# A gated linear attention followed by a snake layer: two stages in a row, against both interleaved chunk by chunk

## The chip, the cores and the metric

The kernel runs on one core of one Trainium2 chip. The metric is the device time of one execution in microseconds (us); an execution is timed as a whole, and a profile of one execution tells what each engine did in it. The engines are TensorE (PE, with its weight loads PEld), VectorE (DVE), ScalarE (ACT), GpSimd (POOL) and SyncE (SP), which here only issues DMAs. Each engine works through its own instructions in order and waits on semaphores that others raise.

## The reference

Inputs are float32: q, k, v and f_logit of 4 batches x 8 heads x 768 positions x 48, and the weights of a layer with 384 inputs and 2048 hidden units. The output is 3072 x 384.

```python
f = 1.0 / (1.0 + np.exp(-f_logit))
for t in range(S):
    state = f[:, :, t, :, None] * state + np.einsum('bhd,bhe->bhde', k[:, :, t], v[:, :, t])
    y[:, :, t] = np.einsum('bhd,bhde->bhe', q[:, :, t], state)
x = np.ascontiguousarray(attn_out.transpose(0, 2, 1, 3)).reshape(B * S, H * D)
h = x @ w_in
s = np.sin(alpha * h)
g = h + s * s / (alpha + 1e-09)
return (g @ w_out).astype(np.float32)
```

The recurrence is computed in chunks of 128 positions. With G the running product of f inside the chunk (exp of a running sum of logarithms), q is multiplied by G and k by 1/G; inside the chunk the result is a masked product of the two with v, and what came before enters through a 48 x 48 state per head that is carried from chunk to chunk.

## The kernel before

It runs two stages one after the other, with a DRAM scratch between them.

**Stage one, attention** (lines 80 to 160). Six chunks, each with all 32 heads (4 batches x 8) side by side. Per chunk, four loads of 768 KB bring f, v, q and k, positions on the partitions. ACT takes the sigmoid (L102) and its logarithm (L104). PE forms the running sums with a triangular mask, 512 columns at a time (L112), DVE copies them out (L113), ACT takes exp of plus and minus the sums (L116, L118), DVE multiplies q and k (L120, L122). A product with a column of ones (L127) and an exp (L128) give each head's decay over the chunk. Then a loop runs over the 32 heads: two transposes (L137, L141) that DVE copies out (L139, L143), the product of k and q (L146) that DVE masks (L148), two products that add up in one PSUM bank (L151 with v, L152 with the state), a DVE copy (L154) and a DMA of 12 KB into the scratch (L155), and the new state (L158, then DVE L159, L160). Each of these instructions serves a single head, so it uses 48 of the 128 rows or columns of the array and short rows on DVE.

**Stage two, the snake layer** (lines 162 to 196). Three DMAs bring the scratch back as x, transposed (L172). Six blocks of 512 tokens follow, each with 16 hidden blocks `fb` of 128 units: three matmuls of 512 columns make `h_ps` (L182, four PSUM buffers), ACT takes the sine with alpha as a per-partition scale (L186) and the square with 1/sqrt(alpha) as scale (L187), DVE adds h (L189), and four matmuls of 384 columns add up the four output tiles (L191). At the block's end DVE copies these out (L195) and SP stores them (L196).

The weights are loaded whole and cast to bf16 by DVE before stage one starts (L74 to L78). The order of the work on each engine is set by the framework's scheduler, from the order of the code and the buffers that are free. A pool's `bufs` is the number of buffers that a tile's name rotates through: a tile can be written only once the readers of the one that had the buffer are done.

## Time and profile before

| what | us |
|---|---|
| time, median of 2 runs (493.24 and 493.69) | 493.47 |
| span of the profiled execution, first to last instruction | 490.3 |
| PE busy in it | 389.7 |
| DVE busy | 316.4 |
| ACT busy | 207.6 |
| POOL busy | 1.1 |

The span is what the rows of a trace add up to; the execution's time has some 3 us around it. The busy times are sums over stages that differ: in the first about 24 us nothing but the weights is loaded and cast, until 332 us stage one runs, until 343 us x is read back, and the rest is stage two. An engine's busy time over the whole span therefore says little, and the stages have to be read one by one. A busy PE is one that has some matmul in flight, not one at its peak.

### The profile page before, as it was taken

The page shows a single profiled execution, that of the slowest core. Times are in us where ns is not written, and L with a number is a line of the kernel's source. Part 1 is how long each engine was busy: PE and PEld are TensorE (multiplying, and loading weights), DVE is VectorE, ACT ScalarE, POOL GpSimd, SP SyncE. Part 2 cuts the span into 40 slices and gives each one's busy share as a digit, 9 for nine tenths or more (in the row PEclk, how much of TensorE's full clock was granted, in tenths as well). Part 3 has the DMA queues.
Part 4 walks back from the last instruction along what each step waited for, and adds up shares of the span by engine and source line. Part 5 has one row for each costly group of instructions (what it writes and reads, how often), then busy time and mean ns, then how long its engine had stood idle before and what let it go on. Part 6 is the DMA issues. An engine that isn't in the chain of part 4 may idle for free.

```text
span 490.3 us, 6888 instructions
## 1 busy us (share of the span) xinstructions
PE 389.7 (79%) x2016; PEld 189.6 (39%) x2034; DVE 316.4 (65%) x1343; ACT 207.6 (42%) x429; POOL 1.1 (0%) x9
## 2 busy tenths in 40 slices
PE   0004999499949994999499959994799999999994
PEld 0002544344425442554255434541344444444441
DVE  1515888688867886788678868881346565555553
ACT  1057303621075105300500040000799999999993
POOL 0000000000000000000000000000000000000000
PEclk9999999999999999999999999999999999999998
DMA  8699558947586642500000000005001010110101
GB/s 281 233 183 187 83 87 135 132 74 127 89 143 104 98 76 51 91 11 12 4 10 10 13 4 10 12 11 197 0 0 66 1 66 0 66 44 22 49 17 65
DMA packets 119430, 35.07 MB, mean 72 GB/s; under 512 B 113504, under 2 KB 118624, under 8 KB 119008
## 3 DMA queue, kind: packets, MB, share of 16 engines
q1 hardware_dynamic: 119392, 34.63, 36.1%
q8 instruction: 16, 0.26, 0.2%
q14 instruction: 22, 0.18, 0.1%
HBM read 27.53 MB, written 7.08 MB: 71 GB/s over the span
## 4 chain that ended last, share of the span: by engine, by line
PE 58%; ACT 18%; issue 8%; DVE 7%; DMA 7%; SPq 0%; DVEq 0%; ACTq 0%
PE y_ps L151 10%; PE y_ps L152 9%; PE kT_ps L141 9%; PE at_ps L146 8%; ACT s_sb L186 7%; PE out_ps L191 7%; PE sc_ps L158 5%; PE qT_ps L137 4%; DMA wtmp_out<-in_moe_w_out_dram 4%; PE h_ps L182 3%; ACT Gl L128 3%; PE glps L127 3%; DVE g_bf L189 3%; ACT s_sb L187 2%; ACT Gi L116 2%
## 5 line engine op out<-in xcount | busy, mean ns | idle before, releaser
L189 DVE TENSOR_TENSOR g_bf<-h_ps,s_sb 128x512 bf16<-128x512 f32 x96 | 65.7, 691 | 73.5 <-ACT s_sb L187 70.0
L191 PE MATMUL out_ps<-w_out_bf,g_bf 128*128 128x384 bf16 x384 | 79.9, 332 | 9.2 <-DVE g_bf L189 7.7
L182 PE MATMUL h_ps<-xT_all,w_in_bf 128*128 128x512 bf16 x275 | 77.9, 391 | 7.1 <-issue 4.7
L154 DVE CAST yt<-y_ps 48x128 bf16<-48x128 f32 x192 | 54.3, 283 | 37.9 <-PE y_ps L152 37.9
L187 ACT ACTIVATE s_sb<-s_sb,alpha_rs 128x512 f32<-128x512 f32 x96 | 69.0, 722 | 3.0
L186 ACT ACTIVATE s_sb<-h_ps,alpha_sb 128x512 f32<-128x512 f32 x96 | 64.5, 674 | 9.8 <-PE h_ps L182 8.8
L137 PE MATMUL qT_ps<-ident,qh 128*48 128x128 bf16 x192 | 59.7, 311 | 1.6 <-DVE qh L120 1.4
L141 PE MATMUL kT_ps<-ident,kh 128*48 128x128 bf16 x192 | 57.9, 301 | 1.3 <-DVE kh L122 1.3
L152 PE MATMUL y_ps<-qtb,state 48*48 48x128 bf16 x192 | 57.4, 299 | 0.0
L146 PE MATMUL at_ps<-qtb,ktb 48*128 48x128 bf16 x192 | 54.9, 286 | 0.2
L151 PE MATMUL y_ps<-at,vt_bf 128*48 128x128 bf16 x192 | 50.9, 265 | 4.0 <-DVE at L148 3.3
L148 DVE TENSOR_TENSOR at<-at_ps,mask 128x128 bf16<-128x128 f32 x192 | 53.2, 277 | 1.1 <-PE at_ps L146 1.1
L191 PEld LDWEIGHTS <-g_bf 128*128 128x128 bf16 x384 | 30.7, 98 | 59.0 <-DVE g_bf L189 45.3
L127 PE MATMUL glps<-ones_c,ft_bf 128*48 128x1 bf16 x192 | 23.3, 168 | 30.8 <-ACT Gl L128 29.9
L128 ACT ACTIVATE Gl<-glps 48x1 f32<-48x1 f32 x192 | 22.5, 158 | 55.9 <-DVE state L160 39.4
L139 DVE COPY qtb<-qT_ps 48x128 bf16<-48x128 bf16 x192 | 39.8, 207 | 8.5 <-PE glps L127 5.6
L152 PEld LDWEIGHTS <-state 48*48 48x48 bf16 x192 | 21.5, 112 | 56.1 <-issue 55.7
L160 DVE TENSOR_SCALAR state<-state,Gl 48x48 bf16<-48x48 bf16 x192 | 42.4, 221 | 0.1
L128 ACT ACT_TABLE_LOAD x6 | 7.7, 1283 | 80.9 <-DVE state L160 80.8
L182 PEld LDWEIGHTS <-w_in_bf 128*128 128x128 bf16 x288 | 28.8, 100 | 33.7 <-issue 10.8
L143 DVE COPY ktb<-kT_ps 48x128 bf16<-48x128 bf16 x192 | 40.3, 210 | 0.7 <-PE kT_ps L141 0.4
L112 PE MATMUL gps<-ft_bf,mask 128*128 128x512 bf16 x13 | 7.5, 593 | 40.6 <-ACT ft_bf L104 35.8
(36 smaller groups left out, 326.5 us busy)
## 6 DMA issues: line engine op xcount, KB each, us to landing
ft<-in_f_logit_dram SPq DMA_DIRECT2D x6, 768.0 KB, 6.2
vt<-in_v_dram SPq DMA_DIRECT2D x6, 768.0 KB, 6.9
qt<-in_q_dram SPq DMA_DIRECT2D x6, 768.0 KB, 6.2
kt<-in_k_dram SPq DMA_DIRECT2D x6, 768.0 KB, 5.8
out_dram<-o_sb SPq DMA_DIRECT2D x24, 192.0 KB, 1.9
wtmp_in<-in_moe_w_in_dram SPq DMA_DIRECT2D x1, 3072.0 KB, 11.0
wtmp_out<-in_moe_w_out_dram SPq DMA_DIRECT2D x1, 3072.0 KB, 18.1
hgrn_x_scratch<-yt SPq DMA_DIRECT2D x192, 12.0 KB, 1.4
```

Source lines behind the costliest of these rows:

```text
L137: nc.tensor.transpose(qT_ps[:D, :], qh[:, bh, :], ident)
L141: nc.tensor.transpose(kT_ps[:D, :], kh[:, bh, :], ident)
L146: nc.tensor.matmul(at_ps[:, :C], ktb, qtb, start=True, stop=True)
L148: nc.vector.tensor_mul(at, at_ps[:, :C], mask)
L151: nc.tensor.matmul(y_ps[:D, :C], vtb, at, start=True, stop=False)
L152: nc.tensor.matmul(y_ps[:D, :C], stt, qtb, start=False, stop=True)
L154: nc.vector.tensor_copy(yt, y_ps[:D, :C])
L182: nc.tensor.matmul(h_ps, w_in_bf[:, kb, fb * P:(fb + 1) * P], xT_all[:, kb, tb * TBLK:(tb + 1) * TBLK], start=(kb == 0), stop=(kb == KB - 1))
L186: nc.scalar.activation(out=s_sb, in_=h_ps, func=Act.Sin, scale=a_sc)
L187: nc.scalar.activation(out=s_sb, in_=s_sb, func=Act.Square, scale=ai_sc)
L189: nc.vector.tensor_add(g_bf, h_ps, s_sb)
L191: nc.tensor.matmul(out_ps4[i], g_bf[:, i * P:(i + 1) * P], wout_tile, start=(fb == 0), stop=(fb == FB - 1))
```

## The change

The two stages become one loop over the six chunks. A chunk now has 128 positions of each of the 4 batches, which are 512 tokens, the size of a block of the layer.

- **Loads** are per unit of two batches (16 heads, 384 KB each of f, k, q, v), two units to a chunk, four buffers for each.
- **`pre(u)`** prepares a unit: ACT takes exp(-f) and the logarithm of one plus it (`L112`, `L113` of the changed kernel), PE sums it for eight heads at a time and puts the four per-pair decay columns beside it in the same bank (L118, L120), ACT takes both exponentials out of that bank (L124, L126), and POOL multiplies q and k and casts v (L128, L130, L114).
- **`attend(c, b)`** does the eight heads of one batch: heads stand in pairs, each padded from 48 to 64 columns, so eight transposes fill one PSUM bank and DVE empties it with one copy (L154); the masked products take two banks and two DVE instructions (L164), y one bank and two (L181, L182), the four pairs' states one (L195). The old state enters its update through a product with the identity (L187). Heads 6 and 7 of y go to a side tile `y3`, which six small DMAs put into x (L202). x stays in SBUF; the scratch is gone.
- **`mlp(c, between)`** is the layer on chunk c. Alpha is multiplied into w_in by DVE (L240) and its reciprocal into w_out by POOL (L244), so the sine and the square need no scale. Odd `fb` are squared by POOL (L265), even ones by ACT (L267). `h` has two PSUM buffers where it had four; the four output tiles are made two at a time in two banks, the second half from the 16 kept `g` tiles. The four `attend` of chunk c+1 are written between its blocks.
- After `mlp(c)` follow the two `pre` of chunk c+2. ACT keeps the order of the code (`manual_schedule`), the other engines are ordered by the scheduler. A table set with both exp and ln is loaded at the start.

```diff
-    x_scratch = nc.dram_tensor("hgrn2_x_scratch", (H, D, B, S), BF16, kind="Internal").ap()
...
-            nc.scalar.activation(out=ft, in_=ft, func=Act.Sigmoid)
-            nc.scalar.activation(out=ft_bf, in_=ft, func=Act.Ln)
...
-                h_ps = psm.tile([P, TBLK], F32, tag="hps", bufs=4)
-                nc.scalar.activation(out=s_sb, in_=h_ps, func=Act.Sin, scale=a_sc)
-                nc.scalar.activation(out=s_sb, in_=s_sb, func=Act.Square, scale=ai_sc)
...
+    ps_o = pool("ps_o", 1, space=bass.MemoryType.PSUM)
+    ps_h = pool("ps_h", 2, space=bass.MemoryType.PSUM)
+    ps_a = pool("ps_a", 4, space=bass.MemoryType.PSUM)
+    ctx.enter_context(tc.manual_schedule(engines={mybir.EngineType.Activation}))
+    nc.scalar.preload_act_table_set("natural_log_exp_and_others")
...
+    def pre(u):
+        nc.scalar.activation(out=ft, in_=ft, func=Act.Exp, scale=-1.0)
+        nc.scalar.activation(out=lf[:, :, :D], in_=ft, func=Act.Ln, bias=1.0)
+        nc.gpsimd.tensor_copy(vb[:, :, :D], vt)
+        for i in range(2):
+            nc.tensor.matmul(cs[:, :H * D], mask, lf[:, i * H:(i + 1) * H, :D], start=True, stop=True)
+            for p in range(HP):
+                nc.tensor.matmul(cs[:, H * D + p:H * D + p + 1],
...
+            nc.scalar.activation(out=G, in_=cs[:, :H * D + HP], func=Act.Exp, scale=-1.0)
+            nc.scalar.activation(out=Gi, in_=cs[:, :H * D], func=Act.Exp)
+            nc.gpsimd.tensor_mul(qh[:, hs, :D], qt[:, hs, :],
...
+            nc.gpsimd.tensor_mul(kh[:, hs, :D], kt[:, hs, :],
...
+    def attend(c, b):
+        for j, src in enumerate((kh, qh)):
+            for p in range(HP):
+                nc.tensor.transpose(tp[:, j * HP + p, :],
...
+        nc.vector.tensor_copy(tr, tp)
+        for p in range(HP):
+            for r in range(2):
+                rs = slice(r * E, (r + 1) * E)
+                nc.tensor.matmul(a_ps[r][:, p, :], tr[rs, p, :], tr[rs, HP + p, :], start=True, stop=True)
+        for r in range(2):
+            nc.vector.tensor_mul(a, a_ps[r], mask4)
...
+                    nc.tensor.matmul(y[rs, p, :], st_old[rs, p, :], tr[rs, HP + p, :],
...
+                nc.tensor.matmul(y[rs, p, :], vb[:, i * H + 2 * p + r, :], at[r][:, p, :],
...
+        nc.vector.tensor_copy(xT[:, :, ts], y[:, :KB, :])
+        nc.vector.tensor_copy(y3[:, ts], y[:, KB, :])
+                nc.tensor.matmul(kv, ident, st_old, start=True, stop=False, skip_group_check=True)
...
+                    nc.tensor.matmul(kv[rs, p, :], kh[:, hh, :], vb[:, hh, :],
...
+        if b == B - 1:
+            for r in range(2):
+                for j in range(KB):
+                    nc.sync.dma_start(out=xT[r * E + D:(r + 1) * E, j, :],
...
+        pre(0)
+        pre(1)
+        attend(0, 0)
+        attend(0, 1)
+        for g4 in range(4):
+            for j in range(KB):
+                nc.vector.tensor_mul(w_in_bf[:, j, cs_], wi[:, j, cs_], al_bc[:, cs_])
+        attend(0, 2)
+        attend(0, 3)
+        for fb in range(FB):
+            nc.gpsimd.tensor_scalar(w_out_bf[:, fb, :], wo[:, fb, :], al_r[:, fb:fb + 1], 1.0,
...
+        pre(2)
+        pre(3)
...
+        def first(fb):
+            h = ps_h.tile([P, TOK], F32, tag="h", name=f"h_{c}_{fb}")
+            for kb in range(KB):
+                nc.tensor.matmul(h, w_in_bf[:, kb, fb * P:(fb + 1) * P], xT[:, kb, :],
+                                 start=(kb == 0), stop=(kb == KB - 1))
+            nc.scalar.activation(out=s, in_=h, func=Act.Sin)
+            if fb % 2:
+                nc.gpsimd.tensor_mul(s2, s, s)
+            else:
+                nc.scalar.activation(out=s2, in_=s, func=Act.Square)
+            nc.vector.tensor_add(g, h, s2)
...
+        for fb in range(FB):
+            first(fb)
+            if fb >= 3:
+                second(os, 0, fb - 3)
+            if fb in (9, 14):
+                between.pop(0)()
...
+        for fb in range(FB):
+            second(os, 1, fb)
+            if fb in (2, 8):
+                between.pop(0)()
+        store(os, 1)
...
+        mlp(c, between)
+        if c + 2 < NCH:
+            pre(2 * c + 4)
+            pre(2 * c + 5)
```

The order of the instructions shows the change best at two places. The first is ACT. Before, it passes from the last chunk's attention into the layer once, with one table load ahead of the first sine (`Gl` is a head's decay, `s_sb` the sine and then its square):

```order
L116 ACTIVATE Gi<-glog 128x1536
L128 ACTIVATE Gl<-glps 48x1 x2
L118 ACTIVATE glog<-glog 128x1536
L128 ACTIVATE Gl<-glps 48x1 x20
L186 ACT_TABLE_LOAD
L186 ACTIVATE s_sb<-h_ps,alpha_sb 128x512 x2
L187 ACTIVATE s_sb<-s_sb,alpha_rs 128x512 x2
```

Now it passes between them at every chunk. Here ACT goes from the last sine of the second chunk through the first unit's `pre` into that of the next (`s_15` is the last sine, `f` a unit's gate, `lf` its logarithm, `cs` the sums):

```order
L262 ACTIVATE s_15_1366<-h_15_1362 128x512
L112 ACT_TABLE_LOAD
L112 ACTIVATE f_1056<-f_1056 128x768
L113 ACT_TABLE_LOAD
L113 ACTIVATE lf_92<-f_1056 128x16x48
L124 ACT_TABLE_LOAD
L124 ACTIVATE G_0_1553<-cs_0_1547 128x388
L126 ACTIVATE Gi_0_1555<-cs_0_1547 128x384
L124 ACTIVATE G_1_1565<-cs_1_1559 128x388
L126 ACTIVATE Gi_1_1567<-cs_1_1559 128x384
L112 ACTIVATE f_1064<-f_1064 128x768
L113 ACT_TABLE_LOAD
```

Three table loads stand in the first unit of the pair and two in the second, and one ahead of the next sine: six at each passage, and 26 in the program, where there were 20 (the set loaded at the start serves the first four units alone).

The second place is DVE, in the loop over heads. Before, six short instructions serve one head, in the order of the next rows, which repeats for each of the 192 head chunks:

```order
L154 CAST yt<-y_ps 48x128
L159 TENSOR_TENSOR state_109<-state_109,sc_ps 48x48
L148 TENSOR_TENSOR at<-at_ps,mask 128x128
L160 TENSOR_SCALAR state_109<-state_109,Gl 48x48
L143 COPY ktb<-kT_ps 48x128
L139 COPY qtb<-qT_ps 48x128
```

Now six longer ones serve eight heads, and the layer's additions (`g_0` to `g_4` here) stand among them. This is the start of the third chunk's layer, with `attend` of the fourth chunk's batches 0 and 1:

```order
L154 COPY tr_0_1741<-tp_0_1732 128x1024
L164 TENSOR_TENSOR at_0_0_1753<-aps_0_0_1743,mask_82 128x512
L164 TENSOR_TENSOR at_0_1_1755<-aps_0_1_1744,mask_82 128x512
L195 TENSOR_TENSOR st_0_1786<-kv_0_1776,G_0_1553 128x256
L154 COPY tr_1_1857<-tp_1_1848 128x1024
L269 TENSOR_TENSOR g_0_1624<-h_0_1616,s_2_0_1622 128x512
L269 TENSOR_TENSOR g_1_1634<-h_1_1626,s_2_1_1632 128x512
L181 CAST xT_1730<-y_0_1757 128x3x128
L182 CAST y_3_1731<-y_0_1757 128x128
L164 TENSOR_TENSOR at_1_0_1869<-aps_1_0_1859,mask_82 128x512
L269 TENSOR_TENSOR g_2_1644<-h_2_1636,s_2_2_1642 128x512
```

The additions of the first two blocks of the layer moved behind the whole of batch 0 and the transposes of batch 1, and the later ones alternate with the attention's instructions. On PE the same holds: at this passage it has the 32 matmuls of the second output half, the sums of the first unit, `h` of blocks 0 and 1, the sums of the second unit, then all of batch 0 and the first half of batch 1, and only then `h` of block 2.

More of the change, by code (lines that the diff above doesn't have):

```diff
@@ L49 @@
     ff = f_logit.rearrange("b h s d -> (b h) s d")
[L51 to L56 removed]
+    pool = lambda name, bufs, **kw: ctx.enter_context(tc.tile_pool(name=name, bufs=bufs, **kw))
+    consts = pool("consts", 1)
+    ld = pool("ld", 4)
```

277 lines of the change are left out of this document (151 added, 126 removed).

## The prediction

> **What bounds the kernel now.** I read the page first: the busy slices and the chain that ended last; then the busy times by stage; then the timeline inside each stage.
>
> ```profile
> span 490.3 us, 6888 instructions
> ...
> PE   0004999499949994999499959994799999999994
> ...
> DVE  1515888688867886788678868881346565555553
> ACT  1057303621075105300500040000799999999993
> ...
> PE 58%; ACT 18%; issue 8%; DVE 7%; DMA 7%; SPq 0%; DVEq 0%; ACTq 0%
> ```
>
> ```profile
> 0.00:30.10 30.10, 0.00 (x0) 0.10 (x1) 8.05 (x35) 1.50 (x2) 1.13 (x9) 1.00 0.83 242
> ...
> 131.00:332.00 201.00, 172.06 (x921) 88.16 (x923) 156.39 (x811) 41.87 (x148) 0.00 (x0) 1.00 0.25 40
> 332.00:343.00 11.00, 4.41 (x11) 1.49 (x12) 0.62 (x3) 0.00 (x0) 0.00 (x0) 1.00 0.63 218
> ...
> 352.00:490.00 138.00, 125.69 (x631) 55.53 (x641) 74.51 (x116) 120.00 (x183) 0.00 (x0) 0.99 0.10 35
> ```
>
> (Columns: stretch, then PE, PEld, DVE, ACT, POOL busy, clock, DMA share, GB/s.) Some 300 of the 490 us are attention, where ACT is busy a fifth of the time; 11 us are the way through DRAM; 147 us are the layer, bound by ACT at 120 of 138 us. POOL does nothing. In the attention stage PE and DVE hand one head to each other in a beat of 1.18 us (L141 to L141):
>
> ```profile
> 100.08 0.30 PE L141 MATMUL kT_ps<-ident,kh 128*48 128x128 bf16 x1
> 100.17 0.31 PE L137 MATMUL qT_ps<-ident,qh 128*48 128x128 bf16 x1
> ...
> 100.62 0.27 PE L151 MATMUL y_ps<-at,vt_bf 128*48 128x128 bf16 x1
> ...
> 100.81 0.30 PE L152 MATMUL y_ps<-qtb,state 48*48 48x128 bf16 x1
> ...
> 101.26 0.30 PE L141 MATMUL kT_ps<-ident,kh 128*48 128x128 bf16 x1
> ```
>
> 192 heads at 1.18 us are 227 us; the rest of the 300 is the preparation of six chunks. Two small matmuls start 0.09 us apart (the transposes) to 0.19 (L151, L152): the bounds for one in the new kernel.
>
> **Prices.**
>
> ```profile
> L187 ACT ACTIVATE s_sb<-s_sb,alpha_rs 128x512 f32<-128x512 f32 x96 | 69.0, 722 | 3.0
> L189 DVE TENSOR_TENSOR g_bf<-h_ps,s_sb 128x512 bf16<-128x512 f32 x96 | 65.7, 691 | 73.5 <-ACT s_sb L187 70.0 <-PE out_ps L191 3.5
> L186 ACT ACTIVATE s_sb<-h_ps,alpha_sb 128x512 f32<-128x512 f32 x96 | 64.5, 674 | 9.8 <-PE h_ps L182 8.8 <-PE out_ps L191 0.9
> L195 DVE COPY o_sb<-out_ps 128x384 f32<-128x384 f32 x24 | 12.2, 551 | 3.8 <-PE out_ps L191 2.6 <-DMA out_dram<-o_sb 1.2
> L113 DVE COPY glog<-gps 128x512 f32<-128x512 f32 x18 | 11.9, 684 | 1.7 <-PE gps L112 1.4
> L122 DVE TENSOR_TENSOR kh<-kt,Gi 128x1536 bf16<-128x1536 f32 x6 | 10.5, 1756 | 13.5 <-ACT Gi L116 13.5
> L116 ACT ACTIVATE Gi<-glog 128x1536 f32<-128x1536 f32 x6 | 8.8, 1471 | 0.0
> L59 POOL TENSOR_SCALAR_AFFINE_SELECT ident<-ident 128x128 bf16<-128x128 bf16 x1 | 0.3, 293 | 0.0
> L182 PE MATMUL h_ps<-xT_all,w_in_bf 128*128 128x512 bf16 x275 | 77.9, 391 | 7.1 <-issue 4.7
> L112 PE MATMUL gps<-ft_bf,mask 128*128 128x512 bf16 x13 | 7.5, 593 | 40.6 <-ACT ft_bf L104 35.8 <-DVE yt L154 3.8 <-DVE glog L113 0.7
> ```
>
> ACT: 128x512 costs 0.67 to 0.72 with a scale per partition, 128x1536 without one 1.47. Between them lie 0.85 for 768 columns, 0.55 for 384, and 0.65 for the sine without its scale. DVE out of PSUM: 384 columns 0.55 and 512 columns 0.68 give 1.04 ns a column and 0.15 besides, so 1.22 for the 1024-column copy, 0.69 for a mask, 0.42 for a state, 0.55 and 0.29 for y. POOL has no two-input row. From below, DVE's rate (1.756 us for 1536) gives 0.59 for 512 columns; from above, twice the affine select's rate for two inputs, 2.3. The nearest row is the affine select itself, on the same engine: 2.3 ns a column, hence 1.17 for a square and 0.88 for 384 columns, which I take.
>
> ```profile
> 346.99 2.74 PE L191 MATMUL out_ps<-w_out_bf,g_bf 128*128 128x384 bf16 x8 [2.74 <-DVE g_bf L189]
> ...
> 353.16 0.82 PE L191 MATMUL out_ps<-w_out_bf,g_bf 128*128 128x384 bf16 x4
> ...
> 357.34 0.81 PE L182 MATMUL h_ps<-xT_all,w_in_bf 128*128 128x512 bf16 x3
> ```
>
> Four output matmuls in 0.82 with the last one's 0.33 are 0.165 each; three `h` matmuls take PE 0.65 and are there after 0.81. A small matmul I take at 0.10, nearer the transposes, since most now stand in rows of eight alike.
>
> ```profile
> 31.44 1.48 ACT L102 ACTIVATE ft<-ft 128x1536 f32<-128x1536 f32 x1
> 32.94 1.28 ACT L104 ACT_TABLE_LOAD   x1
> 34.23 1.48 ACT L104 ACTIVATE ft_bf<-ft 128x1536 bf16<-128x1536 f32 x1
> ```
>
> A table load costs 1.28 and fits between its neighbours with 0.02 us to spare. The Trainium skill ("ScalarE: Activation LUTs", What ACT_TABLE_LOAD costs) adds a drain of about 1.38 us to each switch; the rows here have no room for one. By the page the 24 loads of the four passages below would add 33 us to the sum.
>
> **The change, part by part.**
>
> *Start.* DMA rates:
>
> ```profile
> 3.00:12.00 9.00, 0.00 (x0) 0.00 (x0) 0.25 (x1) 0.21 (x1) 0.00 (x0) 1.00 1.01 371
> ...
> 40.00:50.00 10.00, 5.04 (x37) 3.06 (x36) 5.55 (x14) 8.19 (x27) 0.00 (x0) 1.00 1.45 186
> ```
>
> Weights move at 371 GB/s, the gates (runs of 192 bytes) at 186. The first layer block waits, in PE's order, for the sums of unit 3, whose gate is queued behind three units (1.57 MB, 8.4 us each), the spread alpha (1 MB, 2.8, and 1 for the narrow copy), w_in and w_out (3.1 MB, 8.5 each): 2 + 25.2 + 3.8 + 17 + 2.1 = 50 us. Exp, log and sums: 52.6. Then batch 0 and most of batch 1 of the second chunk stand ahead of `h_0` (8.1 us as below, and 1.5 of state work): 62.2. Until block 2 another batch's transposes, copy, products and state follow (6.8), and `h_2`: its sine starts at 70. The first chunk's attention, the twelve w_in products on DVE and the sixteen w_out products on POOL lie under the DMAs; if they outlasted them, the cost would be their excess.
>
> *The layer loop, blocks 2 to 15.* With two `h` buffers, block n+2 may start only when block n's addition is done. For an odd block that is h 0.81 + sine 0.65 + POOL 1.17 + addition 0.69 and three or four handovers of 0.05: 3.5 us for two blocks, where ACT's own work is 2.0, and the even chain 3.0. The batches written between put into PE some 105 small matmuls (1.6 us a pair beside 2.0 of its own) and into DVE up to 1.22 at a time ahead of an addition: followed by hand, the first pairs take 3.9 and the rest 3.5. I take 3.9, since DVE's and PE's queues are in order and each delay is handed on; 6.5 pairs and a last sine are 26 us. Before, 16 blocks took 22.9 (output copy to output copy), 2.9 a pair: the layer alone gets slower, and pays for the attention that it covers.
>
> ```profile
> 393.05 1.01 DVE o_sb L195 x2
> ...
> 415.96 1.01 DVE o_sb L195 x2
> ```
>
> *The passage between chunks*, from the end of the last sine (0): POOL squares (1.2), DVE adds (1.95), PE ends the first half, DVE copies it out of the two banks that the second half needs (3.3), 32 matmuls (8.6), sums of the first unit (9.3). ACT has done three loads, exp and log by 5.5 and waits. Then 4 x 0.55 (11.5), exp (12.3), load, log (14.5), load (15.8), 4 x 0.55 (18.0), load (19.3), sines of blocks 0 and 1 and a square (21.3). PE has the second sums at 15.2, then batch 0: transposes 16.2, copy 17.4, products 18.4, masks 19.8, state matmuls 19.9, transposes of batch 1 and y 21.4; DVE: state 20.2, copy 22.2; PE: products and three of the state, 23.3; `h_2`, sine at 24.1. POOL's eight products (7 us, from 9.9) end before they are needed. The x DMAs, queued on SP behind the next loads and the output stores, start at about 4 and take 1.4 as the scratch stores did; they end under the 32 matmuls. Passage: 24 us, and with the loop 50 a round.
>
> ```profile
> hgrn_x_scratch<-yt SPq DMA_DIRECT2D x192, 12.0 KB, 1.4
> ...
> out_dram<-o_sb SPq DMA_DIRECT2D x24, 192.0 KB, 1.9
> ```
>
> *Ends.* After the fifth chunk no unit is left to prepare: its last sine to the next first one is 8.6 + 0.8 = 9.4. The sixth chunk has no batches beside it: eight pairs at 3.5, 28. Tail: first half out 1.7, 32 matmuls 5.3, two copies 1.1, store 1.9: 10.
>
> *Sum:* 70 + 4 x 50 + 26 + 9.4 + 28 + 10 = 343.4, against the span of 490.3. The median of the runs, 493.5, lies 3.2 above that span; with them the forecast is 347 us, 0.70 of the time before. The DRAM way (11 us) and the one-head beat (227) go; what is late next is the two-buffer chain and, at each passage, ACT's and PE's turns in series.
>
> **The rivals.**
>
> *B, PE becomes the bound.* At 0.2 us a small matmul (L151 to L152) a round has 184 of them, 36.8, and 20.8 of layer matmuls; with some 5 us in which PE must wait for ACT, 62. Start 72, loop of the fifth chunk 38: 72 + 248 + 38 + 10 + 28 + 10 = 406, time 409. For it: the spacing in the beat. Against it: there PE also waited for DVE.
>
> *C, the chains are shorter.* If POOL runs at DVE's rate the even chain sets 3.0 (3.4 beside batches, 22 a loop), and if pairs on different halves of the array overlap, the passage loses 2.5: 68 + 4 x 43.5 + 22 + 9 + 24 + 10 = 307, time 310. No row shows such an overlap; none excludes it.
>
> *D, the clock of PE halves: slower than before.* The eight matmuls at 346.99, after a wait, take 0.34 each against 0.165 later, though the clock column reads 1.00; L112, after a wait at each chunk, takes 593 ns where the same 512 columns take 391 in the layer. So PE runs at half speed after a pause. The passage has a pause of 3.9 us (10.6 to 14.5). Were PE slow throughout, layer matmuls 41 and small ones 36.8 plus 3 of waiting make 81 a round: 72 + 324 + 60 + 12 + 45 + 12 = 525. It decides from rounds of about 75 us. Against it: the transposes at 0.09 us in the old beat, and PE 78% busy by the new sum. I expect a slow stretch of some us after the pause, within the 0.4 a pair. The Trainium skill ("TensorE: Matmul & The Clock Gate", Part 1) has the same two speeds, and about 3.4 us of idling as what brings the slow one back; the rows agree on the ratio, and nothing here shows the limit.
>
> *E, the overlap fails:* the batches inside the loop are not hidden, and each of 2.6 adds its chain of 7 us: rounds of 68, 26 + 18 in the fifth loop: 70 + 272 + 44 + 9.4 + 28 + 10 = 433, time 437. For it: in-order queues on both sides. Against it: the order alternates them.
>
> *F, each table load with the page's drain:* 347 + 33 = 380.
>
> **How the numbers follow.** Forecast 0.57, B 0.18, C 0.14, E 0.05, D 0.03, F 0.02, and 0.01 for a result near the old time from several of these. The range 300 to 410 leaves out E, D, the last case and the far sides of B and C, together 2 in 10; the forecast's own range is 325 to 372 (a pair at 3.5 to 4.3, 13 us up or down over 5 loops; a passage at 22 to 27, 8 to 12 over four). Faster by over 2%, about what a measurement of this kernel can tell from no change, are all but D and the last: 0.96; within 2% 0.01; slower 0.03.
>
> **What would show it.** Right: first sine at 62 to 66 us, six table loads of 1.28 at each of four passages, 20 to 27 us from a last sine to the third one after, loop pairs of 3.5 to 4.3 us in which `h` waits for the addition two blocks earlier, POOL squares near 1.2 us, no scratch DMA. Wrong: rows of eight small matmuls spaced 0.2 us (B), `h` matmuls at 0.43 us inside the loop (D), a first sine after 75 us, or POOL instructions over 2 us.

## The result, and the profile after

The changed kernel takes 326.54 us (median of 2 runs, 325.58 and 327.50) where the kernel before takes 493.47: a ratio of 0.6622, 95% interval 0.6571 to 0.6673. The prediction was 347 us with a range of 300 to 410. The profiled execution took 325.58 us, 1.7 more than its span.

The page of the changed kernel, its span, busy times and three rows of its slices:

```profile
span 323.9 us, 4521 instructions
...
PE 212.4 (66%) x1683; PEld 114.4 (35%) x1704; DVE 159.7 (49%) x286; ACT 159.1 (49%) x242; POOL 116.1 (36%) x133
...
PE   1156101088866579887599876898795988676655
...
ACT  4310022125557685566945596755649455145420
...
PEclk9999999999999959999869999699978799999999
```

Nothing is busy throughout: PE's digits fall to 5 or 6 at passages between chunks, and PE has little to do in the first eight slices. The chain of waits on this page covers a few per cent of the span, so the stages have to be read one by one. Busy time by stage (stretch, its length, then PE, PEld, DVE, ACT, POOL, granted clock, DMA share, GB/s). The stretches end at sines: start until the sine of block 2; the first loop to its last sine's end; the third loop; the passage behind it; the passage without `pre`; the sixth chunk's sines:

```profile
0.00:78.61 78.61, 24.79 (x293) 16.28 (x294) 33.68 (x65) 17.60 (x30) 30.28 (x46) 1.00 1.13 192
78.61:101.04 22.43, 17.43 (x116) 8.37 (x118) 13.67 (x24) 12.77 (x21) 7.76 (x8) 1.00 0.90 139
166.43:188.76 22.33, 20.20 (x166) 10.14 (x166) 16.02 (x28) 12.65 (x21) 7.05 (x7) 0.99 0.33 44
188.76:209.77 21.01, 15.01 (x132) 8.87 (x129) 8.11 (x16) 15.95 (x22) 10.56 (x11) 0.84 0.12 43
277.26:286.30 9.04, 6.58 (x39) 3.77 (x40) 2.58 (x5) 0.00 (x1) 1.04 (x1) 1.00 0.16 54
286.30:311.77 25.47, 15.87 (x73) 7.04 (x73) 10.05 (x16) 14.47 (x24) 7.27 (x7) 1.00 0.05 16
```

The start waits for DMAs (share 1.13, no engine half busy). A loop takes 22.3 us whatever PE has in it. A passage costs as much as a loop. The groups of instructions that carry this (busy, mean ns of one, idle before and what ended it):

```profile
L262 ACT ACTIVATE s<-h 128x512 f32<-128x512 f32 x96 | 57.1, 595 | 77.2 <-PE h L259 68.4
L259 PE MATMUL h<-xT,w_in_bf 128*128 128x512 bf16 x267 | 77.2, 387 | 25.4 <-DVE g L269 23.2
L265 POOL TENSOR_TENSOR s<-s 128x512 f32<-128x512 f32 x48 | 49.9, 1039 | 114.2 <-ACT s L262 70.9
L269 DVE TENSOR_TENSOR g<-h,s 128x512 bf16<-128x512 f32 x96 | 65.3, 688 | 51.1 <-POOL s L265 44.2
...
L154 DVE COPY tr<-tp 128x1024 bf16<-128x1024 bf16 x24 | 16.4, 685 | 55.0 <-PE tp L150 55.0
...
L112 ACT ACTIVATE f<-f 128x768 f32<-128x768 f32 x12 | 10.2, 850 | 49.4 <-DMA f<-in_f_logit_dram 49.3
```

The first four wait for each other in a ring: ACT for PE, POOL for ACT, DVE for POOL, PE for DVE. The timeline of the sixth chunk, which has no attention beside it, shows one turn of the ring for an odd block:

```profile
293.38 0.81 PE L259 MATMUL h<-xT,w_in_bf 128*128 128x512 bf16 x3 [0.97 <-DVE g L269]
...
294.22 0.60 ACT L262 ACTIVATE s<-h 128x512 f32<-128x512 f32 x1 [0.79 <-PE h L259]
...
294.95 1.04 POOL L265 TENSOR_TENSOR s<-s 128x512 f32<-128x512 f32 x1 [2.35 <-ACT s L262]
...
296.02 1.29 DVE L269 TENSOR_TENSOR g<-h,s 128x512 bf16<-128x512 f32 x2 [1.86 <-POOL s L265]
...
296.76 0.81 PE L259 MATMUL h<-xT,w_in_bf 128*128 128x512 bf16 x3 [1.28 <-DVE g L269]
```

From matmul to matmul in the same bank it is 3.38 us, and in that time two blocks pass, since there are two banks: 3.14 us of it are the four instructions, and the handovers between them take 0.03 to 0.13 each. The passage behind the third loop on ACT:

```profile
188.77 1.28 ACT L112 ACT_TABLE_LOAD   x1
190.07 0.84 ACT L112 ACTIVATE f<-f 128x768 f32<-128x768 f32 x1
...
193.08 1.28 ACT L124 ACT_TABLE_LOAD   x1
197.33 0.49 ACT L124 ACTIVATE G<-cs 128x388 f32<-128x388 f32 x1 [2.97 <-PE cs L120]
...
198.84 0.86 ACT L112 ACTIVATE f<-f 128x768 f32<-128x768 f32 x1
199.72 1.28 ACT L113 ACT_TABLE_LOAD   x1
...
204.83 1.28 ACT L262 ACT_TABLE_LOAD   x1
206.12 0.60 ACT L262 ACTIVATE s<-h 128x512 f32<-128x512 f32 x1
```

ACT waits 2.97 us while PE ends its 32 output matmuls. From the sums on, ACT is busy without a gap until the first sine, 17.36 us after the last one.

### The profile page after: what moved, and what is told of

Its sections match the earlier page's. It is cut to its first block, busy times and chain, and to the rows that moved or that the text cites. A ratio compares the mean times of both kernels' runs of the same rounds, so it can differ in the third digit from the quotient of the medians.

```text
span 323.9 us, 4521 instructions
## 1 busy us (share of the span) xinstructions
PE 212.4 (66%) x1683; PEld 114.4 (35%) x1704; DVE 159.7 (49%) x286; ACT 159.1 (49%) x242; POOL 116.1 (36%) x133
## 5 line engine op out<-in xcount | busy, mean ns | idle before, releaser
L262 ACT ACTIVATE s<-h 128x512 f32<-128x512 f32 x96 | 57.1, 595 | 77.2 <-PE h L259 68.4
L259 PE MATMUL h<-xT,w_in_bf 128*128 128x512 bf16 x267 | 77.2, 387 | 25.4 <-DVE g L269 23.2
L265 POOL TENSOR_TENSOR s<-s 128x512 f32<-128x512 f32 x48 | 49.9, 1039 | 114.2 <-ACT s L262 70.9
L269 DVE TENSOR_TENSOR g<-h,s 128x512 bf16<-128x512 f32 x96 | 65.3, 688 | 51.1 <-POOL s L265 44.2
L275 PE MATMUL o<-w_out_bf,g 128*128 128x384 bf16 x384 | 79.7, 332 | 11.5 <-DVE g L269 8.9
L275 PEld LDWEIGHTS <-g 128*128 128x128 bf16 x384 | 37.2, 99 | 47.8 <-DVE g L269 10.7
L118 PE MATMUL cs<-lf,mask 128*128 128x384 bf16 x24 | 8.9, 401 | 56.9 <-ACT lf L113 56.9
L154 DVE COPY tr<-tp 128x1024 bf16<-128x1024 bf16 x24 | 16.4, 685 | 55.0 <-PE tp L150 55.0
L128 POOL TENSOR_TENSOR qh<-q,G 128x384 bf16<-128x384 f32 x24 | 23.8, 997 | 46.2 <-ACT G L124 39.2
L164 DVE TENSOR_TENSOR at<-aps,mask 128x512 bf16<-128x512 f32 x48 | 31.9, 683 | 9.8 <-PE aps L160 9.8
L130 POOL TENSOR_TENSOR kh<-k,Gi 128x384 bf16<-128x384 f32 x24 | 23.8, 997 | 34.3 <-ACT Gi L126 34.3
L112 ACT ACTIVATE f<-f 128x768 f32<-128x768 f32 x12 | 10.2, 850 | 49.4 <-DMA f<-in_f_logit_dram 49.3
L267 ACT ACTIVATE s<-s 128x512 f32<-128x512 f32 x48 | 30.2, 630 | 1.5
L120 PEld LDWEIGHTS <-lf 128*128 128x128 bf16 x96 | 6.0, 106 | 58.7 <-issue 57.7
L124 ACT ACTIVATE G<-cs 128x388 f32<-128x388 f32 x24 | 11.9, 498 | 16.2 <-PE cs L120 16.2
L181 DVE CAST xT<-y 128x384 bf16<-128x384 f32 x24 | 13.3, 554 | 6.5 <-PE y L178 6.0
## 6 DMA issues: line engine op xcount, KB each, us to landing
wi<-in_moe_w_in_dram SPq DMA_DIRECT2D x6, 384.0 KB, 11.5
```

The source lines that it names most:

```text
L128: nc.gpsimd.tensor_mul(qh[:, hs, :D], qt[:, hs, :], G[:, :H * D].rearrange("c (h d) -> c h d", h=H))
L130: nc.gpsimd.tensor_mul(kh[:, hs, :D], kt[:, hs, :], Gi.rearrange("c (h d) -> c h d", h=H))
L154: nc.vector.tensor_copy(tr, tp)
L164: nc.vector.tensor_mul(a, a_ps[r], mask4)
L259: nc.tensor.matmul(h, w_in_bf[:, kb, fb * P:(fb + 1) * P], xT[:, kb, :], start=(kb == 0), stop=(kb == KB - 1))
L262: nc.scalar.activation(out=s, in_=h, func=Act.Sin)
```

## The experiments

All are edits of the changed kernel, run beside the kernel before (492.9 to 493.6 us). For each, the table gives the median time, its ratio to the kernel before with the 95% interval, and three lengths that add up to the profiled span: until the first sine, four rounds (a round is the mean from one chunk's first sine to the next one's, chunks 1 to 5), and from the fifth chunk's first sine to the end.

| kernel | us | ratio | first sine | round | last two chunks |
|---|---|---|---|---|---|
| the change | 326.5 | 0.6622 (0.6571 to 0.6673) | 75.7 | 43.9 | 72.8 |
| h_three_banks | 311.3 | 0.6312 (0.6285 to 0.6339) | 78.5 | 41.2 | 66.9 |
| squares_on_act | 308.5 | 0.6266 (0.6241 to 0.6291) | 77.1 | 41.8 | 64.4 |
| one_table_load | 320.6 | 0.6493 (0.6465 to 0.6522) | 78.6 | 42.2 | 72.4 |
| w_in_whole | 316.5 | 0.6423 (0.6404 to 0.6441) | 64.9 | 43.7 | 74.8 |
| sums_early | 361.9 | 0.7333 (0.7304 to 0.7362) | 77.7 | 53.8 | 69.1 |
| start_reordered | 334.1 | 0.6775 (0.6753 to 0.6798) | 81.3 | 44.4 | 72.8 |
| one_batch_a_stretch | 303.2 | 0.6149 (0.6111 to 0.6188) | 73.5 | 38.8 | 75.0 |
| all_together | 298.3 | 0.6068 (0.6032 to 0.6103) | 77.6 | 37.4 | 68.2 |
| w_in_two_queues | 328.2 | 0.6656 (0.6621 to 0.6690) | 78.0 | 43.9 | 74.8 |
| no_later_batches | 320.2 | 0.6494 (0.6469 to 0.6519) | 73.3 | 43.7 | 70.7 |
| three_edits | 301.9 | 0.6128 (0.6099 to 0.6156) | 75.1 | 40.0 | 64.2 |
| by_hand_2 | 288.0 | 0.5836 (0.5822 to 0.5850) | 75.2 | 36.4 | 65.5 |

The first sine varies by some 3 us between kernels whose start is the same, so differences of that size in it mean nothing.

### Is the loop the two-bank ring? h_three_banks, squares_on_act

```diff
-    ps_h = pool("ps_h", 2, space=bass.MemoryType.PSUM)
-    ps_a = pool("ps_a", 4, space=bass.MemoryType.PSUM)
+    ps_h = pool("ps_h", 3, space=bass.MemoryType.PSUM)
+    ps_a = pool("ps_a", 3, space=bass.MemoryType.PSUM)
```

> Edit to the changed kernel: `h` gets three banks, the attention's tiles three in place of four. Theory (the loop is the chain PE, sine, square, add, back to PE through two `h` banks): a third bank lets three blocks share one chain of about 3.3 us, so a pair in the sixth chunk, which has no attention beside it, falls from 3.39 us to 2.2 to 2.6, and the sixth chunk from 27.3 to about 20. With the same in the five loops the kernel takes 285 to 305 us, unless the scheduler, which sees another number of banks, moves the batches out of the loops; then the passages get longer by what the loops lose. Rival (PE or DVE throughput bounds the loop): a pair stays at 3.3 to 3.4 us in the sixth chunk, and the time at 325 us or above.

Sines of the sixth chunk on ACT in this kernel, every third of them:

```profile
284.72 0.60 ACT L262 ACTIVATE s<-h 128x512 f32<-128x512 f32 x1 [0.44 <-PE h L259]
...
288.58 0.58 ACT L262 ACTIVATE s<-h 128x512 f32<-128x512 f32 x1
...
292.00 0.60 ACT L262 ACTIVATE s<-h 128x512 f32<-128x512 f32 x1 [0.94 <-PE h L259]
...
295.11 0.58 ACT L262 ACTIVATE s<-h 128x512 f32<-128x512 f32 x1
```

Nine blocks in 10.39 us are 3.46 for three: the ring keeps its length and now serves three blocks, 2.31 us a pair. The sixth chunk, first sine to the end of the span, falls from 37.6 to 30.5 us. The theory holds, and with it the caution in it: at 311 us the whole gains 15 us and not 21 to 41, because the scheduler now puts batches among the 32 output matmuls; of the last two chunks' 72.8 us only 5.9 go, though the sixth alone loses 7.1.

```diff
-            if fb % 2:
-                nc.gpsimd.tensor_mul(s2, s, s)
-            else:
-                nc.scalar.activation(out=s2, in_=s, func=Act.Square)
+            nc.scalar.activation(out=s2, in_=s, func=Act.Square)
```

> Edit to the changed kernel: the odd blocks' squares go from POOL (1.04 us) to ACT (0.63 us), as the even ones. Theory (two-bank chain, its longer half the odd one through POOL): the odd chain loses about 0.4 us, a pair goes from 3.34 to about 2.9 us, over 41 pairs 16 to 18 us: 309 us. First rival (ACT's own work sets the pace): ACT then has four activations a pair, 2.4 us, behind each other; no change or up to 3% slower. Second rival (the attention's instructions in PE's and DVE's queues set the pace): pairs gain nothing in the five loops, only in the sixth chunk, 3 us in all: 323 us.

308.5 us, as the theory said. In the sixth chunk a pair takes 2.88 us, and from one matmul to the next in the same bank it is the same 2.88; in the loops with batches 3.03. The exact hit is in part luck: in the profiled executions the six loops lose 11.5 us, less than the theory's 16 to 18, and another 3.5 go at the passage to the sixth chunk, where the scheduler now puts its first two `h` ahead of the 32 output matmuls.

### What do the batches cost? no_later_batches, sums_early

```diff
-            between = [lambda b=b: attend(c + 1, b) for b in range(B)]
+            between = [lambda: None] * B
...
-        xT, _ = xts.pop(c)
+        xT, _ = xts[0]
```

> The changed kernel without the attention of chunks 1 to 5: their 20 batches (transposes, products, masks, states, x) are left out, and every chunk's layer reads chunk 0's x; the preparations (exp, log, sums, gates, products on POOL) stay. Theory (beside the two-bank chain the batches cost nothing, in the passages the preparation on ACT sets the first sine; only the batch and a half ahead of `h_0` at the start and what stands between the first and the third sine count): loops stay at 22 to 22.6 us, a pair at 3.3 to 3.4, the passages fall from 21.8 to about 20.3, the first sine comes 5 to 8 us earlier, and the kernel takes 308 to 318 us, 20 batches for 9 to 18 us. Rival (the overlap is only partial: a batch costs a good part of the 4.75 us that it takes by itself in the first chunk): 20 batches at 2 us or more, below 285 us.

The passage before the third chunk and its loop, without any batch:

```profile
143.18:164.13 20.95, 9.72 (x63) 5.20 (x62) 4.05 (x7) 15.96 (x21) 11.32 (x12) 0.77 0.62 122
164.13:187.05 22.92, 16.39 (x69) 7.29 (x70) 8.78 (x14) 12.68 (x21) 6.25 (x6) 0.91 0.17 27
```

The loop is no shorter (22.92 against 22.33 us), though DVE has half the work in it; the passage loses half a microsecond (the mean of the four, 0.9). Twenty of the 24 batches cost 6.4 us in all, 0.3 each, even less than the theory gave them. Part of their cost may be masked: without them the granted clock is lower in both stretches, 0.77 and 0.91 where the changed kernel has 0.85 and 0.99. What is left of the loops over heads, 227 us by the prediction's reading of the profile before, is all but hidden.

```diff
         store(os, 0)
+        if c + 2 < NCH:
+            pre(2 * c + 4)
+            pre(2 * c + 5)
         os = outs(1)
...
         mlp(c, between)
-        if c + 2 < NCH:
-            pre(2 * c + 4)
-            pre(2 * c + 5)
```

> Edit to the changed kernel: the two preparations of chunk c+2 stand in the code ahead of the second half's 32 matmuls instead of behind the whole layer. PE's order then has the sums earlier (one unit's ahead of the 32, the other's after 18 of them), and the scheduler draws all four batches of the attention forward into the passage; the loops keep none. Theory (a batch beside the layer's loop costs nothing, since the loop waits for its two `h` banks anyway; in the passage it costs about the 4.75 us from one batch to the next that the first chunk shows): the passages grow by 8 us or more, loops stay at 22 us, and the kernel gets slower though the sums come earlier: 340 to 360 us. Rival (the attention costs the same wherever it stands): the loops shrink by what the passages take, and the earlier sums gain 3 us at each of four passages: 310 to 316 us.

The passage before the third chunk and its loop in this kernel:

```profile
158.19:189.99 31.80, 23.04 (x230) 12.26 (x230) 15.35 (x31) 15.96 (x22) 11.42 (x12) 0.84 0.55 103
189.99:212.31 22.32, 14.54 (x69) 6.40 (x66) 8.99 (x14) 12.76 (x21) 6.25 (x6) 1.00 0.00 1
```

The passage holds 230 matmuls and grows by 10 us; the loop holds 69, no batch, and is as long as before. 361.9 us, slightly worse than the theory's 340 to 360. The same instructions cost nothing at one place and 10 us a round at another.

This kernel also bounds what lying beside the ring is worth. With a single batch in all its loops, where the changed kernel has some ten, it is still 132 us faster than the kernel before; so of the 167 us that the change gains about 35 hang on that place. Another part is that a batch serves eight heads at once: in the first chunk the copies of the transposes start 4.7 us apart, which makes 24 batches 114 us by themselves (an estimate) where the old loops over heads took 227. No run has the batches of eight heads in the old order of two stages, so how the rest is shared stays open.

### Are the table loads on the path? one_table_load

```diff
         if c + 2 < NCH:
+            nc.scalar.preload_act_table_set("natural_log_exp_and_others")
             pre(2 * c + 4)
```

> Edit to the changed kernel: the table set that holds both exp and ln is loaded by hand ahead of each pair of preparations, which leaves 2 table loads at a passage instead of 6. Theory (at a passage ACT's first unit lies under the 32 output matmuls, where ACT waits 2.97 us for PE; only the two loads of the second unit and the one of the sine are on the path): 2 x 1.28 us less at each of four passages, 10 us in all, 316 us; ACT's wait for the first sums grows from 3.0 to about 5.5 us. Rival (every load is on the path): 4 x 1.28 us at each of four passages, 20.5 us, 306 us. Second rival (the loads are hidden altogether): 326 us.

ACT at the passage behind the third loop:

```profile
189.84 0.84 ACT L113 ACTIVATE lf<-f 128x768 bf16<-128x768 f32 x1
196.24 0.49 ACT L124 ACTIVATE G<-cs 128x388 f32<-128x388 f32 x1 [5.55 <-PE cs L120]
```

Its wait for the first sums grows from 2.97 to 5.55 us, by the two loads taken away there. From last to first sine it is 15.27 us in place of 17.36. Until the sine of block 2 the four passages lose 11.1 us together (87.3 to 76.1), as the theory said. The time falls by 5.9 only: 3 us come back in the start, which this edit doesn't touch, and 4 in longer loops.

### What holds up the start? w_in_whole, start_reordered, w_in_two_queues

```diff
         for j in range(KB):
-            for r in range(2):
-                h0 = (2 * j + r) * D
-                nc.sync.dma_start(out=wi[r * E:r * E + D, j, :], in_=moe_w_in[h0:h0 + D, :])
-                h1 = (2 * KB + r) * D + 16 * j
-                nc.sync.dma_start(out=wi[r * E + D:(r + 1) * E, j, :], in_=moe_w_in[h1:h1 + 16, :])
+            nc.sync.dma_start(out=wi[:, j, :], in_=moe_w_in[j * P:(j + 1) * P, :])
```

> Edit to the changed kernel: w_in is loaded by 3 DMAs to all 128 partitions instead of 12 to 48 or 16 partitions each; the rows are then not in the order in which the heads are paired, so the layer computes with permuted weights. Bytes and all else are the same. Theory (a DMA to 48 or 16 partitions runs at 118 to 153 GB/s where one to all 128 runs at 371, and the gate logits of units 2 and 3 wait behind it): the load of 3.1 MB shrinks from about 26 to 9 us, the log gates of unit 3 start near 47 instead of 63.5 us, the first sine near 59 to 63 instead of 75.7 us, and the time is 309 to 314 us. Rival (the start is bound by DVE's and PE's attention work of the first chunk, or by the loads of short runs): the first sine moves by 3 us at most, 323 us or above.

While w_in comes in, the changed kernel, and then this one:

```profile
24.00:42.00 18.00, 6.53 (x80) 4.58 (x80) 13.00 (x27) 0.00 (x0) 0.00 (x0) 1.00 1.03 153
```

```profile
24.00:30.00 6.00, 4.00 (x51) 2.90 (x52) 4.52 (x11) 0.00 (x0) 0.00 (x0) 1.00 1.01 406
```

Pieces for 48 or 16 partitions move at 153 GB/s, whole ones at 406, with the DMA engines equally occupied (shares 1.03 and 1.01). Unit 2's gate is used at 34.4 us in place of 46.9, unit 3's at 51.1 in place of 63.5, and the first sine comes 10.7 us earlier. That is what the start waits for. At 64.9 us the first sine is a little behind the theory's 59 to 63, and so is the time, 316.5.

```diff
+        load(2)
+        load(3)
         for j in range(KB):
             for r in range(2):
+                eng = nc.scalar if r else nc.sync
...
-        load(2)
         wo = wst.tile([P, FB, d_model], F32)
...
-        load(3)
```

> Edit to the changed kernel, start only, output as the reference's: the gates, keys, queries and values of units 2 and 3 are asked for ahead of w_in and w_out, and the 6 pieces of w_in that go to partitions 64 to 127 go through ACT's DMA queue beside those of the lower half on SP's. Theory (the start is the gate logits of unit 3 behind the slow pieces of w_in): unit 3's gate is used near 45 us instead of 63.5, the first sine comes at 55 to 62 us, and the kernel takes 305 to 313 us. Rival (the 16 DMA engines are the bound whatever the order, and the pieces stay as slow): the weights then come last, near 63 us, `h_0` waits for them in place of the gate, and the first sine stays within 4 us of 75.7: 322 us or above.

Slower, 334 us, as the rival has it (322 and above), though the first sine is 5.6 us late where the rival allowed 4. The reordering fails in two ways. ACT stands still while it issues DMAs (the rows ACTq are its issues):

```profile
1.98 0.44 ACTq L223 DMA_DIRECT2D wi<-in_moe_w_in_dram  x1
9.80 0.32 ACTq L225 DMA_DIRECT2D wi<-in_moe_w_in_dram  x1
14.99 0.32 ACTq L223 DMA_DIRECT2D wi<-in_moe_w_in_dram  x1
22.53 0.32 ACTq L225 DMA_DIRECT2D wi<-in_moe_w_in_dram  x1
22.90 0.84 ACT L112 ACTIVATE f<-f 128x768 f32<-128x768 f32 x1 [20.82 <-DMA v<-in_v_dram]
```

Each issue after the third starts 0.02 us after the landing of a load of unit 0 on SP's queue (the gate's at 9.78 us, k's at 14.97, v's at 22.51). In the trace it waits for the very semaphore that this load had: the program's DMAs take turns at eight semaphores. So the first exp comes at 22.9 us in place of 5.0, and unit 3's gate, which has landed at 46.8, is used only at 55.5. And as the rival says, the weights then come last, w_in at 64.3 us. Its products stand among the attention's instructions in DVE's order, the last ones end at 79.8, and the first sine follows at 81.3.

```diff
-                nc.sync.dma_start(out=wi[r * E:r * E + D, j, :], in_=moe_w_in[h0:h0 + D, :])
+        def w_in_half(r, eng):
+            for j in range(KB):
+                eng.dma_start(out=wi[r * E:r * E + D, j, :], in_=moe_w_in[h0:h0 + D, :])
...
+        w_in_half(0, nc.sync)
...
         pre(1)
+        w_in_half(1, nc.scalar)
```

> Edit to the changed kernel, start only, output as the reference's: the 6 pieces of w_in for partitions 64 to 127 are issued by ACT, behind the first two units' exponentials, while SP issues the 6 pieces of the lower half. Theory (pieces that reach few partitions are slow, at 140 to 165 GB/s, and two streams to different halves of the partitions run side by side): w_in is in by about 35 us instead of 45, the gate of unit 2 is used near 35 instead of 46.9, that of unit 3 near 52 instead of 63.5, the first sine comes at 65 to 68, and the kernel takes 313 to 319 us, as with w_in whole (316.5). Rival (the 16 DMA engines themselves are the bound on such pieces): both streams share the rate, the first sine stays at 74 to 79 and the time at 323 to 330 us.

Until 31 us ACT's pieces run beside the spread alpha, which lands 9 us later than in the changed kernel; then both streams of w_in run at once:

```profile
32.30:42.00 9.70, 3.82 (x49) 2.71 (x50) 8.14 (x17) 0.00 (x0) 0.00 (x0) 1.00 1.02 169
```

The rival holds: two streams of such pieces move 169 GB/s together, hardly more than the 153 of one alone, and unit 3's gate is used at 64.1 us. The Trainium skill ("SBUF — State Buffer", Door 1: The DMA port swizzle) gives 196 GB/s for a transfer of 1 MiB to partitions 0 to 63 and 104 for one to 16 partitions; an estimate from these two for pairs of pieces of 384 and 128 KB is 160, which agrees with the 153 here. By the same section partitions 0 to 63 and 64 to 127 have separate ports, but the page goes on ("Can I just issue two DMAs to hit both halves?") that two concurrent DMAs, one to each half, came to only 6% over a single one; the trace agrees in kind, with 169 over 153. The narrow pieces are also smaller than the whole ones (384 and 128 KB against 1 MB), and no run here separates the two, so what makes them slow stays open.

### Is there a better order? one_batch_a_stretch, all_together, three_edits, by_hand_2

```diff
-    ctx.enter_context(tc.manual_schedule(engines={mybir.EngineType.Activation}))
+    ctx.enter_context(tc.manual_schedule(engines={mybir.EngineType.Activation, mybir.EngineType.PE}))
...
+            if fb >= 2:
+                next(batches, None)
...
+            logs(2 * c + 4)
+            logs(2 * c + 5)
...
+            if more and fb == 0:
+                sums(2 * c + 4)
+            if more and fb == 5:
+                sums(2 * c + 5)
+            if c + 1 < NCH and fb in (10, 13):
+                first(c + 1, done)
```

> Edit to the changed kernel: PE's order is written out by hand as ACT's is. Each block from the third on carries one step of the attention (transposes; products; state products; the rest with the next batch's transposes), so that all four batches stand in the loop and none in the passage; exp and ln of both units stand at the loop's end under one table load, the sums at two places among the 32 matmuls, and the first two `h` of the next chunk among them too. Two banks for `h` as before; squares of odd blocks below 7 on ACT, since POOL multiplies q and k then. Theory (the passage is ACT and PE taking turns, the loop is the two-bank chain and has room for all four batches): passage 9 to 12 us instead of 21.8, loop 22 to 25 us, 265 to 285 us in all. Rival (PE is the bound once it no longer waits: 8 us of small matmuls, 16 of `h` and first-half matmuls a loop): the loop grows by most of what the passage loses, 300 us or above.

The third loop and the passage behind it:

```profile
154.92:180.08 25.16, 22.25 (x232) 11.43 (x230) 20.66 (x38) 13.93 (x23) 5.89 (x7) 1.00 0.43 73
180.08:194.38 14.30, 11.00 (x69) 5.71 (x68) 3.77 (x8) 11.46 (x18) 8.73 (x9) 0.88 0.14 49
```

The time, 303.2, is the rival's (300 and above) and misses the theory's 265 to 285. The passages fall to between 12.7 and 14.3 us, and a last sine is followed by the next first one after 9.0 to 10.1. But the loop, with four batches in it, is now 25 us long and PE busy for 22.3 of them; most of the rest are its waits for the copies of the transposes (2.5). So the rival's mechanism, PE as the bound, takes back a third of what the passages lose, where the rival had most of it.

```diff
-    ps_h = pool("ps_h", 2, space=bass.MemoryType.PSUM)
-    ps_a = pool("ps_a", 4, space=bass.MemoryType.PSUM)
+    ps_h = pool("ps_h", 3, space=bass.MemoryType.PSUM)
+    ps_a = pool("ps_a", 3, space=bass.MemoryType.PSUM)
...
+                eng = nc.scalar if r else nc.sync
```

> The kernel of the hand-written PE order, with three banks for `h` (three for the attention's tiles) and the reordered start as well. Theory: the parts add up, since each takes a wait of its own out of the path: start 57 to 62 us, five rounds of 31 to 36 us (PE's own work is then about 29 a round: 16 blocks at 0.98 us, 8 us of small matmuls, 5.3 us for the second half), sixth chunk about 20, tail 10: 245 to 270 us. Rival (the gains overlap, and another engine's queue, DVE with 26 us of work a round or POOL, takes over): no better than the best of the single edits, 290 us or above.

298.3 us, the rival's range (290 and above) and not the theory's 245 to 270. The rounds of 37.4 us are a little above the theory's 31 to 36. Three banks gain little (1.4 us a round) once PE's order sets the pace; the start, which is start_reordered's, gains nothing.

```diff
+            nc.scalar.activation(out=s2, in_=s, func=Act.Square)
...
+            nc.scalar.preload_act_table_set("natural_log_exp_and_others")
...
+        w_in_half(1, nc.scalar)
```

> Three edits at once, the scheduler's order kept: all squares on ACT (308.5 us alone), one table load ahead of the preparations (320.6), w_in by two queues. Theory: they take waits out of three different stretches, the loop, the passage and the start, and add up: 18 + 6 + 10 less than 326.5, 288 to 297 us. Rival (they overlap, ACT being busier in loop and passage alike): 300 us or above.

301.9 us. The squares (18.0 alone) and the table loads (5.9) add up to 302.6, so these two do not overlap, though the time is in the rival's range; the third edit, which gains nothing alone, gains nothing here.

```diff
+    def steps(c):
+        now = stages(c, 0)
+        next(now)
+        yield
+        for b in range(B):
...
+            after = stages(c, b + 1) if b + 1 < B else None
+            if after is not None:
+                next(after)
```

> The hand-written PE order with three banks for `h`, w_in by two queues, and each batch's transposes one step earlier, so that VectorE's copy of them has a whole block's time before PE needs it. Theory (in the hand order PE is the bound, at about 33 us of work in a round of 37.9, and most of the rest is PE waiting 0.7 to 1.2 us for the copy at every batch): a round of 34 to 36 us, start near 66, 265 to 282 us. Rival (DVE's queue, with 26 us a round in a strict order, takes the wait over): rounds stay at 37 us or above, 285 us or above.

288.0 us, the best version here: 0.881 of the changed kernel's time (0.5836 over 0.6622). One round of it, first sine to first sine:

```profile
146.74:183.49 36.75, 32.66 (x290) 16.96 (x294) 23.73 (x44) 25.42 (x41) 15.70 (x17) 0.95 0.42 80
```

PE is busy for 32.7 of 36.8 us. The gain over all_together is 10 us where 16 to 33 were expected: PE's waits for the copy fall from 3.4 to 0.9 us a round, but the mean round is still 36.4 us. PE's busy time does not fall with them: all_together has 32.0 us of it in a round, at a granted clock of 1.00 where this round has 0.95. The rival's numbers fit better, though not its mechanism, since DVE is busy for only 23.7 us of a round. As in the two kernels before, the divided w_in brings nothing.

## Why the prediction was right, and where its terms were off

The sum of the prediction beside the profiled execution:

| term | predicted | measured |
|---|---|---|
| start, until the sine of block 2 | 70 | 78.6 |
| five loops, blocks 2 to 15 | 5 x 26 = 130 | 111.4 (22.1 to 22.4 each) |
| four passages with `pre` | 4 x 24 = 96 | 87.3 (21.0 to 22.9 each) |
| passage after the fifth chunk | 9.4 | 9.0 |
| sixth chunk, to its last addition | 28 | 27.4 |
| tail | 10 | 10.2 |
| around the span | 3.2 | 1.7 |

- **Mechanism.** The forecast's own case came about: the one-head beat and the way through DRAM are gone, and what is late next is "the two-buffer chain and, at each passage, ACT's and PE's turns in series". h_three_banks, squares_on_act and one_table_load each change one of these alone, and the stretch in question follows.
- **Start, mis-sized by 8.6 us.** The prediction let w_in pass at the weights' 371 GB/s, "w_in and w_out (3.1 MB, 8.5 each)". That row was a load to all 128 partitions; the new one goes to 48 and 16 at 153 GB/s, and unit 3's gate is used at 63.5 us where the text has 50. w_in_whole shows it. The first sine at 75.7 is what the text named as a sign of error. Behind the gate it took too much: 20 us to the sine of block 2, where it is 15.1.
- **Loop, mis-sized by 3.7 us each.** "I take 3.9, since DVE's and PE's queues are in order and each delay is handed on" is the step that fails: hardly any delay is handed on. A pair takes 3.2 to 3.3 us with batches and 3.3 without (a fifth of the time from the sine of block 4 to that of block 14), below the 3.5 to 4.3 that the text named as a sign of being right; no_later_batches shows the same from the other side. The batches' price on PE was too high as well: the text puts 1.6 us of small matmuls into a pair, 0.10 each, but in the loop four transposes take 0.39 us and eight products 0.40, which makes it 0.8 (an estimate, at 0.05 each). Without the 0.4 for them the text had 3.5, from a square of 1.17 us (1.04), a sine of 0.65 (0.60) and handovers of about the measured size.
- **Passage, mis-sized by 2.2 us each.** The order of the turns was right step by step, down to the wait before the sums; behind the third loop it takes 21.0 us where the text has 24.1. Four exponentials out of a bank were put at 4 x 0.55; they last 0.50 but start 0.38 apart, 1.5 in all. The copy of eight transposes was put at 1.22 from "1.04 ns a column"; in bf16 its 1024 columns take 685 ns. The 0.10 us for a small matmul holds here for the transposes by luck, because PE is slow in this stretch; the eight products, put at 1.0 us, take 0.61.
- **What was costed at nothing** was nothing: PE waits 0.2 us in all for the x DMAs, and at the passage above its transposes follow the sums without a wait for POOL's products. That two of the six loads at a passage stand in ACT's wait is shown by one_table_load.
- **Rivals.** B (PE the bound, 409 us) did not come: eight small matmuls take 0.40 us in the loop. It is what the hand-written order runs into instead. E (no overlap, 437 us) is refuted by no_later_batches, F (a drain at each load, 380 us) by the rows above, in which an activation follows a load by 0.02 us. C (310 us) was half right. Its condition on POOL failed: the square takes 1.04 us, nearly what the forecast had, and not 0.59. Its condition on pairs held: the eight products, in pairs on different halves of the array, take as long as four transposes on the whole of it. D is there as a slow stretch, and no more. PE in the passage behind the third loop, and then in the loop:

```profile
201.91 0.48 PE L118 MATMUL cs<-lf,mask 128*128 128x384 bf16 x1 [3.03 <-ACT lf L113]
...
202.76 0.59 PE L150 MATMUL tp<-ident,kh 128*128 128x128 bf16 x4
...
204.56 0.61 PE L160 MATMUL aps<-tr 64*128 64x128 bf16 x8 [0.78 <-DVE tr L154]
```

```profile
214.75 0.39 PE L150 MATMUL tp<-ident,qh 128*128 128x128 bf16 x4
...
216.25 0.40 PE L160 MATMUL aps<-tr 64*128 64x128 bf16 x8
```

Behind a wait of 3.03 us four transposes take 0.59 us in place of 0.39 and eight products 0.61 in place of 0.40, and the passage's granted clock is 0.84. The forecast allowed for "a slow stretch of some us after the pause".

The errors have both signs: 8.6 at the start against 18.6 in the loops and 8.7 in the passages, 20 us below the forecast in the end. The forecast's own range was 325 to 372, and 326.5 lies at its very edge. That it lies inside is luck: without the 8.6 us that the start is late, the time would be about 318 (an estimate from these terms).

## What to carry to other kernels

When work of one kind is laid beside a ring of engines that share few buffers, count the ring's length over the number of buffers; what fits into its waits is free, and the same instructions in a stretch without such waits cost their full time. Price a transfer by a row of the same kind (partitions reached, size of a piece), not by its bytes alone. Before more buffers or faster instructions are tried, look at what the next bound is: here PE's own work, 33 of 37 us a round, stands right behind the ring.

## What was unexpected of the hardware

- w_in in pieces for 48 and 16 partitions moved at 153 GB/s, on two queues at once at 169, in whole at 406, with the DMA engines occupied alike.
- Eight small products in pairs on different halves of the array take 0.40 us, as long as four transposes on the whole of it (0.39).
- Activations of 384 columns out of PSUM last 0.48 to 0.51 us but start 0.37 to 0.39 us apart.
- VectorE's copy of 1024 bf16 columns out of PSUM takes 685 ns, as long as an instruction on 512 float32 columns (683 to 688). POOL's product of 384 columns into padded bf16 tiles takes 997 ns, nearly as long as its square of 512 float32 columns (1039).
